# Linear attention followed by a gated MLP: state products paired with scores, normalisations on a second engine, and a new hand-written order

## The chip, the core and the metric

The kernel runs on one core of one Trainium2 chip. The metric is the device time of one execution in microseconds (us). The core's engines work side by side, each through its own list of instructions in order: TensorE (PE, matrix products and transposes into PSUM), VectorE (DVE), ScalarE (ACT), GpSimd (POOL, which has no way to PSUM) and SyncE (SP, which here only issues DMAs). Semaphores hold an instruction back until what it needs is done.

## What is computed

The reference takes q, k, v of 4 batches, 8 heads, 768 positions and 64 channels, and a decay per head, and computes linear attention in blocks of 64 positions; then, on the 512 channels of all heads, an MLP with a spatial gate:

```python
intra = ((qb @ kb.T) * Dmask) @ vb              # Dmask[i, j] = lam**(i-j) for i >= j, else 0
inter = (qb * lam_pow) @ kv_state
out[:, :, sl] = intra + inter
kv_state = lam_block * kv_state + (kb * rev_pow).T @ vb
...
h = np.maximum(x @ w_in, 0.0)                   # 512 -> 1024
u, v = h[..., :512], h[..., 512:]
v_n = (v - mean(v)) / np.sqrt(var(v) + 1e-06)   # per position, over the 512 channels
v_s = einsum('ts,bsd->btd', w_spatial, v_n) + b_spatial[None, :, None]
out = (u * v_s) @ w_out
```

## The kernel before

A batch of 768 positions is cut into three steps of 256; steps are numbered 0 to 11 over the four batches (n // 3 is the batch, n % 3 the step in it), and each step has two blocks of 128 (c = 0, 1). PSUM has eight banks; bank 7 holds the running state, the others are handed out by number.

**The order is written out by hand.** The string ORDER (lines 16 to 81) lists tokens such as `MK.3.1.3.4.D`: an operation, its indices, mostly its PSUM banks, and last the engine: T for TensorE, D for VectorE, A for ScalarE, P for GpSimd, S for SyncE's DMA queue. The loop at lines 526 to 528 issues them one after another, so a token's place in the string fixes its place in its engine's list; waits between engines follow from the data and the banks. Which engine makes a copy or an eviction is therefore a matter of the token's last letter.

The operations that this document speaks of, with the lines that the profile names:

- Loads by SP: LQ, LK, LV (line 190; three buffers each), BS the spatial bias, broadcast (258). Loads by GpSimd, cast to bf16 on the way: WI.0 and WI.1 the halves of w_in (246; WI.0 is the half for v, read by PV), WS.0 and WS.1 (251), WO (255). GT is a tiny copy on GpSimd that waits until a load has landed (242).
- Decay: KM, QM multiply k and q by their decay into bf16 (288); QC, VC only cast (177, 175 or 179, by engine); the last index of KM, QM, QC is the half, or 2 for the whole.
- Transposes: in steps 0 to 4 TK and TQ on PE (318), evicted by EK and EQ; from step 5 on by DMA, DK and DQ (301, 305).
- Scores SC (349): 16 products of 64x64 each for half of the channels, masked by MK on DVE (354). SC, KV and AV are the small products; all others on PE use the full array of 128x128.
- State products KV.n.c (366), 16 products into bank 7; SS copies the state out (177 or 175) before the next KV adds to it.
- Attention output AV.n.c (387 and 396): the part through the state copy, then scores times v. FN is a copy of one element that waits for the first half of AV. EX evicts the result (x) to SBUF.
- Projection: PV (421) gives the v half of a block of 128 positions, evicted with relu by EV; PU (459) gives the u half, evicted by EU.
- Normalisation: BN computes mean and variance on DVE (436, 437); RA takes the root on ACT (441), RD the reciprocal on DVE (446); VN subtracts the mean and scales, 128x512 bf16, on DVE (450).
- Spatial gate: WT transposes w_spatial on PE (471), EW evicts; GP writes the bias into a bank (481, shown at 175 or 177); PW (485) adds six products of 384 columns; GM multiplies by u on DVE (491).
- Output: PO (496), the last block in two halves PH (505), evicted by EO and EH, stored by ST and SH (519, 515).

The work of a batch overlaps the next: while the PW and PO of one batch run, the attention of the next batch is threaded between them.

Of the kernel before, what the change touches and what calls it, by code (L numbers as in the profile page):

```python
# [21 lines left out]
TK.2.0.6.T QC.2.0.A MK.1.1.0.1.D QC.2.1.D VC.1.A AV.0.0.2.3.T FN.0.2.3.A MK.1.0.4.5.D LV.2.S KV.1.0.T LK.3.S
KM.2.1.P TQ.2.0.0.T AV.1.0.1.4.T FN.1.1.4.A AV.0.1.2.3.T SS.1.0.D AV.1.1.1.4.T EX.1.1.4.A GT.1.2.P WS.1.P
TQ.2.1.5.T KV.1.1.T EX.1.0.1.D EX.0.1.3.D EX.0.0.2.D PV.1.1.4.T GT.2.1.P TK.2.1.1.T PV.0.0.3.T EV.1.1.4.A
EK.2.1.1.D PU.1.0.2.T PV.1.0.4.T LV.3.S BS.S EK.2.0.6.A SS.1.1.D EQ.2.0.0.D VC.2.D BN.1.1.D EQ.2.1.5.D KV.2.0.T
EV.0.0.3.A LQ.3.S BN.0.0.D EV.1.0.4.A SC.2.1.0.1.T EU.1.0.2.A BN.1.0.D RA.1.A SC.2.0.5.6.T MK.2.1.0.1.D KM.3.1.P
RD.1.D LK.4.S PU.0.1.3.T PV.0.1.4.T WT.0.0.2.T MK.2.0.5.6.D EV.0.1.4.A BN.0.1.D PU.1.1.0.T WT.2.0.1.T EU.0.1.3.A
SS.2.0.A AV.2.0.3.4.T RA.0.A EU.1.1.0.A WT.1.0.5.T FN.2.3.4.D AV.2.1.3.4.T LQ.4.S WT.0.1.6.T EW.2.0.1.D
EX.2.0.3.A WT.1.1.1.T EX.2.1.4.D EW.0.0.2.A EW.0.1.6.A PV.2.0.0.T PV.2.1.3.T VN.1.1.D EW.1.1.1.D RD.0.D LV.4.S
VN.0.1.D EW.1.0.5.A WO.P EV.2.0.0.D BN.2.0.D EV.2.1.3.A WT.2.1.4.T KM.3.0.P VC.3.A VN.1.0.D BN.2.1.D KM.4.0.P  # L30
PU.0.0.2.T RA.2.A TK.3.2.1.T GT.2.2.P PU.2.1.6.T VN.0.0.D RD.2.D EW.2.1.4.A KM.4.1.P GP.0.0.0.0.A GP.0.1.0.3.A
LQ.5.S KV.3.0.T VN.2.0.D LK.5.S PU.2.0.5.T VN.2.1.D PW.0.0.0.0.T EU.2.1.6.D GP.0.0.1.6.D EU.0.0.2.A GP.0.2.0.2.A
PW.0.1.0.3.T QC.4.2.P QC.3.2.D EU.2.0.5.D TQ.3.2.4.T PW.0.0.1.6.T EK.3.2.1.A GM.0.0.0.0.D QM.5.1.P PW.0.2.0.2.T
LQ.6.S GP.0.1.1.5.A GM.0.0.1.6.D LV.5.S EQ.3.2.4.D GP.0.3.1.0.A PW.0.3.1.0.T GM.0.1.0.3.D SS.3.0.D PW.0.1.1.5.T
GP.0.3.0.6.A GM.0.2.0.2.D SC.3.1.3.4.T KV.3.1.T GM.0.3.1.0.D MK.3.1.3.4.D SS.3.1.A GP.0.2.1.2.A SC.3.0.0.1.T
PW.0.3.0.6.T LK.6.S MK.3.0.0.1.D VC.4.P PW.0.2.1.2.T QM.5.0.P TQ.4.2.3.T GM.0.3.0.6.D QM.6.1.P TK.4.2.4.T
GM.0.2.1.2.D PO.0.2.0.T AV.3.0.1.6.T EQ.4.2.3.D KM.5.0.P GM.0.1.1.5.D KV.4.0.T EK.4.2.4.A EO.0.2.0.A FN.3.1.6.D
SC.4.0.2.3.T KM.5.1.P SS.4.0.A SC.4.1.4.5.T AV.3.1.1.6.T EX.3.0.1.D KV.4.1.T DQ.5.S MK.4.1.4.5.D EX.3.1.6.A
PO.0.4.0.T PV.3.1.6.T PV.3.0.1.T PO.0.3.4.T EV.3.1.6.A PU.3.0.5.T MK.4.0.2.3.D AV.4.0.2.6.T EV.3.0.1.A
EO.0.4.0.A VC.5.D BN.3.1.D KM.6.1.D FN.4.2.6.A DK.5.S BN.3.0.D SS.4.1.A EU.3.0.5.D LQ.7.S PO.0.5.3.T KM.6.0.P  # L40
LV.6.S EO.0.3.4.A AV.4.1.2.6.T KV.5.0.T EX.4.1.6.D EO.0.5.3.A LK.7.S QM.6.0.P SC.5.0.0.1.T SC.5.1.4.5.T
PO.0.1.3.T EX.4.0.2.A PV.4.1.2.T QM.7.1.P MK.5.0.0.1.D EO.0.1.3.A PV.4.0.6.T RA.3.A LV.7.S MK.5.1.4.5.D
AV.5.0.0.1.T GP.1.0.0.3.D EV.4.0.6.A VC.6.D FN.5.0.1.D SS.5.0.A PO.0.0.4.T KV.6.0.T EV.4.1.2.A AV.5.1.0.1.T
PU.4.1.5.T BN.4.0.D EX.5.1.1.A BN.4.1.D PU.4.0.6.T KM.7.1.D VC.7.D RD.3.D EX.5.0.0.A RA.4.A DQ.6.S DK.6.S
PV.5.1.2.T PV.5.0.1.T RD.4.D VN.4.1.D PU.3.1.0.T EU.4.0.6.A EV.5.1.2.A VN.3.0.D PU.5.1.6.T EU.4.1.5.D VN.4.0.D
QM.7.0.P EV.5.0.1.A BN.5.1.D EO.0.0.4.A BN.5.0.D SS.6.0.A EU.3.1.0.A DQ.7.S RA.5.A KM.7.0.P VN.3.1.D DK.7.S
SC.6.0.1.2.T KV.6.1.T RD.5.D SC.6.1.4.5.T LV.8.S VN.5.0.D VN.5.1.D PU.5.0.0.T LK.8.S EU.5.1.6.A MK.6.1.4.5.D
GP.1.2.1.6.A MK.6.0.1.2.D EU.5.0.0.A KM.8.1.P GP.1.1.1.0.A PW.1.2.1.6.T PW.1.0.0.3.T GP.1.3.1.4.A SS.6.1.D
PW.1.1.1.0.T LQ.8.S SC.7.0.1.2.T GM.1.2.1.6.D GM.1.0.0.3.D GM.1.1.1.0.D AV.6.0.5.6.T FN.6.5.6.D KV.7.0.T LQ.9.S
MK.7.0.1.2.D PW.1.3.1.4.T AV.6.1.5.6.T LK.9.S GP.1.0.1.3.D SS.7.0.A KV.7.1.T EX.6.0.5.A SC.7.1.0.1.T  # L50
PW.1.0.1.3.T QM.8.1.D MK.7.1.0.1.D GP.1.2.0.2.A GP.1.3.0.5.A KM.9.0.D PW.1.2.0.2.T PW.1.3.0.5.T GM.1.0.1.3.D
KM.8.0.P QM.8.0.P SS.7.1.A KM.9.1.P DK.8.S GM.1.2.0.2.D EX.6.1.6.A DQ.8.S GP.1.1.0.0.A GM.1.3.0.5.D LV.9.S
VC.8.A PW.1.1.0.0.T PV.6.0.1.T PV.6.1.6.T GM.1.3.1.4.D EV.6.0.1.A LK.10.S EV.6.1.6.A AV.7.0.2.3.T LK.11.S
SC.8.1.4.5.T GM.1.1.0.0.D SC.8.0.0.1.T FN.7.2.3.A MK.8.1.4.5.D KV.8.0.T AV.7.1.2.3.T EX.7.1.3.D MK.8.0.0.1.D
PO.1.5.6.T ST.0.0.S ST.0.3.S EX.7.0.2.A PU.6.1.4.T PO.1.4.5.T LQ.11.S BN.6.0.D AV.8.0.2.3.T VC.9.P PO.1.0.0.T
FN.8.2.3.D SS.8.0.D KV.9.0.T EO.1.4.5.D AV.8.1.2.3.T KM.10.1.P QM.9.1.D EU.6.1.4.A PV.7.1.1.T LQ.10.S EX.8.0.2.A
BN.6.1.D KM.10.0.P LV.10.S GP.2.3.1.4.D PU.7.1.5.T PV.7.0.2.T EV.7.1.1.D BN.7.1.D EX.8.1.3.A QM.9.0.P PV.8.0.3.T
RA.6.A RD.6.D DK.9.S EV.7.0.2.A EO.1.0.0.A PU.8.1.1.T SS.9.0.A PV.8.1.2.T EV.8.0.3.A VN.6.0.D BN.7.0.D
EV.8.1.2.A EO.1.5.6.A BN.8.0.D RA.7.A KV.9.1.T PU.6.0.0.T BN.8.1.D DQ.9.S VN.6.1.D GP.2.0.1.3.A QM.10.0.P
EU.6.0.0.A RD.7.D VN.7.1.D VN.7.0.D RA.8.A LV.11.S PO.1.1.2.T RD.8.D PO.1.2.6.T VC.10.P SS.9.1.D VN.8.0.D  # L60
VN.8.1.D QM.11.1.P PU.7.0.0.T QM.10.1.D EU.8.1.1.D EU.7.1.5.A PU.8.0.5.T EU.7.0.0.A EU.8.0.5.A GP.2.1.0.0.D
# [15 lines left out]
GP.3.3.1.4.A GM.3.2.1.0.D ST.2.4.S PW.3.3.1.4.T PW.3.1.1.2.T PW.3.2.0.3.T GP.3.0.0.6.D GM.3.3.1.4.D ST.2.2.S
GM.3.1.1.2.D PW.3.1.0.5.T PW.3.0.0.6.T PH.3.5.1.0.T GM.3.3.0.1.D GM.3.1.0.5.D one.D PO.3.4.4.T EO.3.4.4.A
PO.3.3.2.T GM.3.0.0.6.D GM.3.2.0.3.D ST.3.4.S EH.3.5.1.0.D PH.3.5.0.1.T EH.3.5.0.1.D EO.3.3.2.A PO.3.1.5.T
EO.3.1.5.D PO.3.0.6.T EO.3.0.6.D SH.3.5.1.S SH.3.5.0.S PO.3.2.3.T ST.3.3.S ST.3.1.S ST.3.0.S EO.3.2.3.A ST.3.2.S  # L80
# [478 lines left out]
```

## Time and profile before

| | |
|---|---|
| median of three runs | 148.28 us (147.71 to 148.53) |
| the profiled execution | 148.72 us, its span 147.0 us |
| mean granted TensorE clock | 0.971 |
| busy: PE, DVE, ACT, POOL | 130.0, 117.4, 75.7, 46.0 us |
| largest groups on PE | PW 33.0, PU 24.3, PV 23.9, PO 21.5 us |
| largest on DVE | MK 28.5, GM 16.4, BN 16.4, VN 10.9 us |
| HBM read, written | 24.77 MB, 6.29 MB |

The page gives one execution as the hardware profiler recorded it, times counted from its first instruction. A group line reads: source line, engine, operation, output<-inputs, shapes, count | busy time in us, mean ns of one | idle time of the engine just ahead of them and what ended it. The chain of waits goes back from the last instruction, at each step to what released it; a piece of it reads start, length, what. A line of waits reads: who waited, for whom, us in total, times, the longest. Helpers hide their callers: line 175 is every copy on ACT, 177 every copy on DVE, 426 and 428 every relu.

### The profile page before, as it was taken

The page shows a single profiled execution, that of the slowest core. Times are in us where ns is not written, and L with a number is a line of the kernel's source. Part 1 is how long each engine was busy: PE and PEld are TensorE (multiplying, and loading weights), DVE is VectorE, ACT ScalarE, POOL GpSimd, SP SyncE. Part 2 cuts the span into 40 slices and gives each one's busy share as a digit, 9 for nine tenths or more (in the row PEclk, how much of TensorE's full clock was granted, in tenths as well). Part 3 has the DMA queues.
Part 4 walks back from the last instruction along what each step waited for, and adds up shares of the span by engine and source line. Part 5 has one row for each costly group of instructions (what it writes and reads, how often), then busy time and mean ns, then how long its engine had stood idle before and what let it go on. Part 6 is the DMA issues. An engine that isn't in the chain of part 4 may idle for free.

```text
span 147.0 us, 4585 instructions
## 1 busy us (share of the span) xinstructions
PE 130.0 (88%) x1929; PEld 84.2 (57%) x1946; DVE 117.4 (80%) x229; ACT 75.7 (51%) x154; POOL 46.0 (31%) x57
## 2 busy tenths in 40 slices
PE   1077599999999999999999999996999899999990
PEld 1056364676766756477665656663664555865540
DVE  1289956799978789989997799899978779997640
ACT  3968323679862546468637414764506473580021
POOL 7669600240188670520048075373000000000000
PEclk9999955999999999999999999999999999999997
DMA  3999999999999677998995899992987386011065
GB/s 88 346 347 347 259 215 218 216 318 238 310 311 339 185 91 203 347 202 183 321 333 148 215 355 336 221 216 81 165 263 76 143 337 236 2 72 75 0 235 193
DMA packets 58374, 32.27 MB, mean 220 GB/s; under 512 B 15858, under 2 KB 55282, under 8 KB 58354
## 3 DMA queue, kind: packets, MB, share of 16 engines
q1 hardware_dynamic: 55968, 29.23, 73.0%
q0 software_dynamic: 2384, 2.75, 10.7%
q8 instruction: 15, 0.25, 0.7%
q14 instruction: 5, 0.04, 0.1%
q10 hardware_dynamic: 2, 0.00, 0.0%
HBM read 24.77 MB, written 6.29 MB: 211 GB/s over the span
## 4 chain that ended last, share of the span: by engine, by line
PE 80%; DMA 7%; SPq 5%; DVE 3%; issue 2%; ACT 1%; DVEq 0%
PE ps L485 22%; PE ps L459 15%; PE ps L421 14%; PE ps L496 12%; SPq L190 5%; DMA q_in<-in_q_dram 4%; PE ps L396 4%; PE ps L349 4%; PE ps L366 3%; PE ps L387 3%; DMA qT<-qc 3%; DVE a_sb L354 2%; PE ps L318 2%; PE ps L471 2%; PE ps L505 1%
## 5 line engine op out<-in xcount | busy, mean ns | idle before, releaser
L485 PE MATMUL ps<-wt_sb,vn 128*128 128x384 bf16 x192 | 33.0, 326 | 1.3 <-ACT ps L175 1.3
L354 DVE TENSOR_TENSOR a_sb<-ps,m 128x1024 bf16<-128x1024 f32 x24 | 28.5, 1214 | 2.8 <-PE ps L349 2.5
L288 POOL TENSOR_TENSOR kc<-k_in,lv 128x512 bf16<-128x512 f32 x17 | 19.0, 1131 | 35.2 <-DMA k_in<-in_k_dram 24.0
L485 PEld LDWEIGHTS <-vn 128*128 128x128 bf16 x192 | 18.3, 98 | 13.3 <-issue 1.5
L421 PE MATMUL ps<-win_sb,xT 128*128 128x512 bf16 x90 | 23.9, 399 | 0.7 <-issue 0.6
L459 PE MATMUL ps<-xT,win_sb 128*128 128x256 bf16 x192 | 24.3, 275 | 0.0
L496 PE MATMUL ps<-wout_sb,gT 128*128 128x512 bf16 x81 | 21.5, 380 | 0.8 <-issue 0.3
L459 PEld LDWEIGHTS <-win_sb 128*128 128x128 bf16 x192 | 18.5, 99 | 5.0 <-DMA win_sb<-in_moe_w_in_dram 0.6
L426 ACT ACTIVATE vh<-ps 128x512 bf16<-128x512 f32 x20 | 12.0, 599 | 14.6 <-PE ps L421 14.6
L491 DVE TENSOR_TENSOR gT<-ps,uT 128x384 bf16<-128x384 f32 x32 | 16.4, 547 | 3.1 <-PE ps L485 3.1
L175 ACT ACTIVATE o_sb<-ps 128x512 f32<-128x512 f32 x19 | 11.1, 593 | 14.4 <-PE ps L496 14.4
L436 DVE BATCH_NORM_STATS2 st<-vh 128x6 f32<-128x512 bf16 x24 | 16.4, 682 | 1.3 <-ACT vh L426 1.2
L288 POOL TENSOR_TENSOR qc<-q_in,lqn 128x512 bf16<-128x512 f32 x11 | 11.9, 1087 | 12.2 <-DMA q_in<-in_q_dram 5.1
L175 ACT ACTIVATE xT<-ps 128x512 bf16<-128x512 f32 x16 | 9.2, 596 | 11.6 <-PE ps L396 11.2
L421 PEld LDWEIGHTS <-xT 128*128 128x128 bf16 x96 | 9.4, 101 | 9.9 <-issue 0.8
L175 ACT ACTIVATE ps<-bsp 128x384 f32<-128x384 f32 x23 | 11.0, 491 | 5.3 <-DVE uT L428 2.7
L496 PEld LDWEIGHTS <-gT 128*128 128x128 bf16 x92 | 8.2, 98 | 8.2
L426 ACT ACTIVATE uT<-ps 128x512 bf16<-128x512 f32 x16 | 9.5, 593 | 4.2 <-PE ps L459 4.2
L450 DVE TENSOR_SCALAR vn<-vh,mv,rstd 128x512 bf16<-128x512 bf16 x24 | 10.9, 476 | 0.3
L396 PE MATMUL ps<-a_sb,vb 64*64 64x128 bf16 x384 | 10.2, 221 | 0.3 <-DVE a_sb L354 0.3
L349 PE MATMUL ps<-qT,kT 64*64 64x128 bf16 x384 | 9.2, 219 | 1.2 <-DVE a_sb L354 0.8
L366 PE MATMUL ps<-vb,kc 64*64 64x64 bf16 x320 | 8.7, 196 | 0.4 <-ACT seen L175 0.4
(70 smaller groups left out, 156.1 us busy)
## 6 DMA issues: line engine op xcount, KB each, us to landing
q_in<-in_q_dram SPq DMA_DIRECT2D x12, 512.0 KB, 6.6
k_in<-in_k_dram SPq DMA_DIRECT2D x12, 512.0 KB, 6.2
v_in<-in_v_dram SPq DMA_DIRECT2D x12, 512.0 KB, 6.0
out_dram<-o_sb SPq DMA_DIRECT2D x23, 256.0 KB, 2.8
wsp_raw<-in_moe_w_spatial_dram POOLq DMA_DIRECT2D x2, 576.0 KB, 15.9
win_sb<-in_moe_w_in_dram POOLq DMA_DIRECT2D x2, 512.0 KB, 11.4
wout_sb<-in_moe_w_out_dram POOLq DMA_DIRECT2D x1, 512.0 KB, 9.1
bsp<-in_moe_b_spatial_dram SPq DMA_DIRECT2D x1, 384.0 KB, 17.9
```

The source lines that it names most:

```text
L175: nc.scalar.activation(out=o, in_=i, func=AF.Copy)
L288: vec(e).tensor_tensor(out=dst[n % NCA][:, u].rearrange("p u m o d -> p o (u m) d"), in0=src[n % NIN].rearrange("p (o u) m d -> p o u m d" ...
L349: nc.tensor.matmul(out=pa[o][row(c), w, j], lhsT=kT[n % NTR][row(o), u, j, c * Q64:(c + 1) * Q64], rhs=qv(n, o, u, c), start=(w == 0 and j ...
L354: nc.vector.tensor_tensor(out=a_sb[n % NA][:, i].rearrange("p o w j x -> p o w (j x)"), in0=ps[:, b0:b1 + 1:b1 - b0].rearrange("p o (w y) ...
L396: nc.tensor.matmul(out=po[c ^ o][row(w), c, i], lhsT=vb[n % NCA][row(c), 4 * o + u, j, :], rhs=a[row(c), i, o, w, j, :], start=(r == 0 and ...
L421: nc.tensor.matmul(out=bank(b), lhsT=x[:, slot(c, g)], rhs=win_sb[:, g, DH:DFF], start=(g == 0), stop=(g == NCH - 1))
L426: nc.scalar.activation(out=o, in_=i, func=AF.Relu)
L436: nc.vector.bn_stats(out=st6[p2][:, t], in_=vh[p2][:, t])
L459: nc.tensor.matmul(out=pu[:, f2].rearrange("p (c x) -> p c x", c=2), lhsT=win_sb[:, g, f * P:(f + 1) * P], rhs=x[:, slot(0, g):slot(1, g) ...
L485: nc.tensor.matmul(out=bank(b)[:, 0:HW], lhsT=vn[bb % 2][:, s, f * P:(f + 1) * P], rhs=wt_sb[:, s, i * HW:(i + 1) * HW], start=False, stop ...
L491: nc.vector.tensor_tensor(out=gT[bb % 2][:, f, cols], in0=bank(b)[:, 0:HW], in1=uT[bb % 2][:, f, cols], op=ALU.mult)
L496: nc.tensor.matmul(out=bank(b), lhsT=gT[bb % 2][:, f, t * P:(t + 1) * P], rhs=wout_sb[:, f, :], start=(f == 0), stop=(f == NCH - 1))
```

## The change

Four things are edited.

1. A new operation KS takes the place of KV.n.0, KV.n.1 and one SC in steps 3, 4, 6, 7, 9 and 10. KS.n.c issues the 16 state products of block c and, between them, 8 of the 16 scores of channels half 0 (those that read the other half of the rows, o = 1 - c), so that two KS of a step replace two KV and SC.n.0.
2. VN gets a form for ACT: an activation with func Identity, scale rstd and bias shift, where shift = -mean * rstd comes from a new small operation NB on DVE (two values per partition and step). Eleven of the 24 VN go to ACT, 13 stay on DVE; eight NB are added.
3. f_l is rewritten: four products of the identity matrix with itself into a bank that is free. It was in the kernel before, but ORDER did not call it; now FL stands twice in the first steps. The memset of ones (token one, near the end) goes; its tile is renamed and no longer used.
4. ORDER is written anew throughout. Besides the places, engines change: five GP, three EV, two EO, two EK, two QC and one EW more on DVE; four VC, two EU, two EX, two SS, both EH and one QM fewer on it.

```diff
+    shift = many(2, [P, NT], FP32, "shift")
...
-    def f_l(e, k, w, b, new):
-        for i in range(k):
-            nc.tensor.matmul(out=bank(b)[:, 0:w], lhsT=ones[:, 0:P], rhs=ones[:, 0:w],
-                             start=(new == 1 and i == 0), stop=True, skip_group_check=True)
+    def f_l(e, n, b):
+        for i in range(4):
+            nc.tensor.matmul(out=bank(b)[:, 0:P], lhsT=ident, rhs=ident, start=True, stop=True)
...
+    def k_s(e, n, c, b0, b1):
+        pkv = bank(SB)[:, 0:4 * D].rearrange("p (u d) -> p u d", u=4)
+        new = n % NR == 0 and c == 0
+        o = 1 - c
+        ps_c = bank((b0, b1)[o]).rearrange("p (w j x) -> p w j x", w=2, j=2)
+
+        def state(u, m):
+            for h in range(2):
+                nc.tensor.matmul(out=pkv[row(h), u], lhsT=kc[n % NCA][row(c), u, m, h, :],
+                                 rhs=vb[n % NCA][row(c), 4 * h + u, m, :],
+                                 start=new and u == 0 and m == 0, stop=(u == 3 and m == 1),
+                                 skip_group_check=True)
+
+        for u in range(4):
+            w, j = divmod(u, 2)
+            for x in range(2):
+                nc.tensor.matmul(out=ps_c[row(x), w, j], lhsT=kT[n % NTR][row(o), w, j, x * Q64:(x + 1) * Q64],
+                                 rhs=qv(n, o, w, x), start=(u == 0), stop=(u == 3), skip_group_check=True)
+            state(u, 0)
+            state(u, 1)
...
+    def n_b(e, n):
+        r, p2 = n % NR, n // NR % 2
+        ts = slice(2 * r, 2 * r + 2)
+        nc.vector.scalar_tensor_tensor(out=shift[p2][:, ts], in0=mv[p2][:, ts, 0], scalar=-1.0,
+                                       in1=rstd[p2][:, ts], op0=ALU.mult, op1=ALU.mult)
+
     def v_n(e, n, c):
         t, p2 = 2 * (n % NR) + c, n // NR % 2
-        vec(e).tensor_scalar(out=vn[p2][:, t], in0=vh[p2][:, t], scalar1=mv[p2][:, t, 0:1],
-                             scalar2=rstd[p2][:, t:t + 1], op0=ALU.subtract, op1=ALU.mult)
+        if e == "A":
+            nc.scalar.activation(out=vn[p2][:, t], in_=vh[p2][:, t], func=AF.Identity,
+                                 bias=shift[p2][:, t:t + 1], scale=rstd[p2][:, t:t + 1])
+        else:
+            vec(e).tensor_scalar(out=vn[p2][:, t], in0=vh[p2][:, t], scalar1=mv[p2][:, t, 0:1],
+                                 scalar2=rstd[p2][:, t:t + 1], op0=ALU.subtract, op1=ALU.mult)
```

Of the order, the lists of some engines over the stretches that matter here, first before, then after (engine letters left out):

```text
SP   before  LQ.0 LQ.1 LK.0 LK.1 LV.0 LK.2 LQ.2 LV.1 LV.2 LK.3 LV.3 BS LQ.3 LK.4 LQ.4 LV.4 LQ.5 LK.5 ...
     after   LQ.0 LK.0 LQ.1 LK.1 LV.0 LV.1 LQ.2 LK.2 LV.2 LK.3 BS LK.5 LQ.3 LV.3 LK.4 LQ.4 LV.4 LQ.5 ...
POOL before  msk idn pos posk QC.0.1 QC.1.0 QC.1.1 QC.0.0 KM.1.1 GT.1.1 WI.0 WI.1 WS.0 KM.2.0 KM.2.1 GT.1.2 WS.1 ...
     after   msk idn posk pos QC.0.0 KM.1.0 WI.0 QC.1.1 WS.0 VC.1 GT.1.1 QC.2.1 WI.1 KM.2.0 WS.1 WO ...
PE   before  ... AV.1.1.1.4 TQ.2.1.5 KV.1.1 PV.1.1.4 TK.2.1.1 PV.0.0.3 PU.1.0.2 PV.1.0.4 KV.2.0 SC.2.1.0.1 ...
     after   ... AV.1.1.1.4 PV.0.1.5 FL.15.6 TK.2.1.3 PV.1.1.1 WT.0.0.0 SC.2.0.2.3 PV.1.0.4 PV.0.0.6 SC.2.1.0.1 PU.1.1.5 ...
PE   before  ... PU.2.0.5 PW.0.0.0.0 PW.0.1.0.3 TQ.3.2.4 PW.0.0.1.6 PW.0.2.0.2 PW.0.3.1.0 PW.0.1.1.5 SC.3.1.3.4 KV.3.1 SC.3.0.0.1 ...
     after   ... TK.3.2.6 PW.0.0.0.0 PW.0.2.1.5 TQ.3.2.3 PW.0.1.1.1 KS.3.0.5.6 SC.3.1.2.3 PW.0.3.1.4 PW.0.2.0.0 KS.3.1.5.6 TK.4.2.3 ...
ACT  after   ... RA.5 EU.5.1.3 VN.3.1 VN.5.1 VN.4.0 EU.3.1.3 EU.4.0.0 GP.1.0.0.3 ...
```

More of the change, by code (lines that the diff above doesn't have):

```diff
@@ L22 @@
[L22 to L61, printed above, removed]
@@ L77 @@
[L77 to L80, printed above, removed]
+LQ.0.S lam.A msk.P idn.P LK.0.S LQ.1.S mkc.D QC.0.1.D posk.P pos.P LB.0.T LN.0.A LL.D QC.0.0.P LK.1.S LX.A
@@ L147 @@
     bsp = sb([P, S], FP32, "bsp")
-    ones = sb([P, 512], BF16, "ones")
+    spare = sb([P, 512], BF16, "spare")
     q_in = many(NIN, [P, H, 2, D], FP32, "q_in")
@@ L519, in st_o @@
         eng.dma_start(out=out[bb, t * P:(t + 1) * P, :], in_=o_sb[(bb * NT + t) % NO])
-    ops = dict(GT=after, one=c_ones, FL=f_l, FN=f_n, lam=c_lam, posk=c_posk, pos=c_pos, LB=l_b, LN=l_n, LL=l_l, LX=l_x, LT=l_t, idn=c_ident, msk=c_mask, mkc=c_mask2, WI=w_in, WS=w_sp, WO=w_out, BS=b_sp,
+    ops = dict(GT=after, FL=f_l, FN=f_n, lam=c_lam, posk=c_posk, pos=c_pos, LB=l_b, LN=l_n, LL=l_l, LX=l_x, LT=l_t, idn=c_ident, msk=c_mask, mkc=c_mask2, WI=w_in, WS=w_sp, WO=w_out, BS=b_sp,
                LK=ld_k, LQ=ld_q, LV=ld_v, KM=k_m, QM=q_m, DK=d_k, DQ=d_q, QC=q_c, VC=v_c, TK=t_k, TQ=t_q, EK=e_k, EQ=e_q,
-               SC=s_c, MK=m_k, KV=k_v, SS=s_s, AV=a_v, EX=e_x, PV=p_v, EV=e_v, BN=b_n, RA=r_a, RD=r_d,
+               SC=s_c, MK=m_k, KV=k_v, KS=k_s, SS=s_s, AV=a_v, EX=e_x, PV=p_v, EV=e_v, BN=b_n, RA=r_a, RD=r_d, NB=n_b,
                VN=v_n, PU=p_u, EU=e_u, WT=w_t, EW=e_w, PW=p_w, GP=g_p, GM=g_m, PO=p_o, EO=e_o, ST=st_o, PH=p_h, EH=e_h, SH=s_h)
```

86 lines of the change are left out of this document (64 added, 22 removed).

## The prediction

> **What bounds the kernel now.** I read the page first, then the windows of ten microseconds, then the chain of waits.
>
> ```profile
> span 147.0 us, 4585 instructions
> PE 130.0 (88%) x1929; PEld 84.2 (57%) x1946; DVE 117.4 (80%) x229; ACT 75.7 (51%) x154; POOL 46.0 (31%) x57
> PE   1077599999999999999999999996999899999990
> ```
>
> The last line is the share of busy time in 40 slices of 3.7 us, in tenths: TensorE is idle or thin in the first five and nearly full afterwards. Two windows make that sharp:
>
> ```profile
> 20.00:30.00 10.00, 9.73 (x116) 5.76 (x111) 7.39 (x15) 4.86 (x8) 1.70 (x2) 0.71 1.17 217
> 40.00:140.00 100.00, 97.26 (x1419) 61.48 (x1432) 86.79 (x166) 49.39 (x103) 29.56 (x28) 1.00 0.77 202
> ```
>
> After the window's length stand the busy times of PE, weight loads, DVE, ACT and GpSimd, then PE's granted clock: 0.71 in the stretch from 20 to 30 us. From 40 to 140 us PE rests 2.7 us in 100, while DVE is 87% and ACT 49% busy. So PE is the bound there, and a new order can win at most those 2.7 us, unless PE's work itself becomes cheaper. The chain and the list of waits name where most of it lies:
>
> ```profile
> 98.84 2.07 PE ps L485 x12
> 100.91 0.68 DVE uT L428
> ...
> 101.61 0.50 ACT ps L175
> ...
> 110.33 4.00 DMA qT<-qc
> ```
> ```profile
> PE ps L485 <- ACT ps L175: 1.3, 1, 1.3
> PEld L459 <- DMA win_sb<-in_moe_w_in_dram: 0.6, 1, 0.6
> PE ps L349 <- DMA qT<-qc: 0.4, 1, 0.4
> ```
>
> PW.2.2.1 waits 1.3 us for a bias copy that ACT can make only after a late DVE eviction (EU.8.1), and the scores of step 11 wait 0.4 us for a transposing DMA. The other 1.0 us is scattered. Before 40 us the order of arrival of the inputs counts.
>
> **PE's own work (KS, and the regrouping).** These are the prices, from the chain of waits (start, length, what):
>
> ```profile
> 30.02 0.34 PE ps L471 x6
> ...
> 36.76 0.45 PE ps L318 x8
> 37.21 0.87 PE ps L459 x8
> 38.08 0.37 PE ps L366 x16
> 38.45 0.98 PE ps L459 x8
> ...
> 52.89 1.73 PE ps L421 x8
> ...
> 74.17 0.22 PE ps L396 x16
> 74.39 0.24 PE ps L366 x16
> ...
> 82.85 0.45 PE ps L349 x32
> ```
>
> A KV alone between full 128x128 products takes 0.37 us, inside a run of small 64x64 products 0.24; and the projection that follows takes 0.98 where its like takes 0.87. So each run of small products costs 0.13 + 0.11, about 0.22 us, for going in and out. 16 score products take 0.225 (0.45 for 32).
>
> From the first PW to the end, before has 14 KV, 18 SC and 17 runs of small products; after has 3 KV, 12 SC, 12 KS and 22 runs; the rest is the same piece for piece. A KS holds the 16 products of a KV and 8 scores. The trace has none. Bounds: if scores and states hide each other, the longer of the two, 0.24; if they simply add, 0.24 + 0.11 = 0.35; if every product starts at the pace of the lone KV, 24 x 0.37/16 = 0.56. Scores read one half of the rows and state products the other, as the two halves of an AV do, whose 16 products take 0.22, 14 ns each; that row is the nearest, so I take 0.25. Then: -11 x 0.24 - 6 x 0.225 + 12 x 0.25 = -1.0, and 5 more runs x 0.22 = +1.1. **Sum: +0.1 us**, with ends at -0.0 and +3.8. What the pairing saves, the splitting into more runs pays back.
>
> A KS adds a wait: the second of a step (KS.n.1) needs the state copy SS.n.0 of the first, and holds back half the scores, so MK.n.0 on DVE and whatever PE has queued behind. Between the two stand 0.6 (step 4) to 1.2 us of PE work, against one copy:
>
> ```profile
> L175 ACT ACTIVATE s_sb<-ps 128x256 bf16<-128x256 f32 x12 | 4.6, 379 | 5.2 <-PE ps L366 3.0 <-DVE seen L177 2.2
> L450 DVE TENSOR_SCALAR vn<-vh,mv,rstd 128x512 bf16<-128x512 bf16 x24 | 10.9, 476 | 0.3
> L222 ACT ACTIVATE lq<-posq,llrow 128x256 bf16<-128x256 f32 x12 | 5.0, 495 | 0.0
> L175 ACT ACTIVATE qc<-q_in 128x512 bf16<-128x512 f32 x1 | 0.6, 622 | 0.0
> L177 DVE COPY ps<-bsp 128x384 f32<-128x384 f32 x9 | 5.0, 551 | 0.1
> L177 DVE CAST vb<-v_in 128x1024 bf16<-128x1024 f32 x6 | 4.1, 686 | 1.0 <-DMA v_in<-in_v_dram 0.6 <-issue 0.5
> L428 DVE TENSOR_SCALAR vh<-ps 128x512 bf16<-128x512 f32 x4 | 2.7, 685 | 0.2 <-PE ps L421 0.2
> L436 DVE BATCH_NORM_STATS2 st<-vh 128x6 f32<-128x512 bf16 x24 | 16.4, 682 | 1.3 <-ACT vh L426 1.2
> L441 ACT ACTIVATE rstd<-mv,eps_t 128x2 f32<-128x2 f32 x12 | 3.5, 295 | 2.4 <-DVE mv L437 1.4 <-DVE seen L177 0.8
> ```
>
> 0.38 us and its hand-over fit, except in step 4, where perhaps 0.1 shows.
>
> **Eleven normalisations on ACT, and the other swaps.** A VN on DVE costs 0.476 on average, so DVE loses 5.2 us. On ACT it is a pass over 512 elements (0.62, the qc row) with two operands that differ per partition; one such operand costs about 0.495 - 0.379 = 0.12 (lq against s_sb, 256 elements each), so 0.62 + 0.23 = 0.85 is my estimate, 9.4 us for eleven; bounds 0.62 and 1.0.
>
> The Trainium skill ("ScalarE: Activation LUTs", Rules for kernel authors) says to put multiply and add on VectorE and not on ScalarE, against this edit; from the prices of its section What ACT_TABLE_LOAD costs, 186 ns, 93 for each such operand and 0.833 per element, an estimate is 799 ns, which makes the third rival below a little less likely than my 0.85 does. No row here shows the operation.
>
> Besides, DVE loses four VC (0.686 each, -2.7) and gains five GP (0.551, +2.8) and three EV (0.685, +2.1); the smaller swaps and eight NB (tiny: 0.3 at most, the RA row) come to about -1, so DVE ends some 4 us lighter and ACT about 7 heavier (9.4 less the five GP and three EV, plus small ones), 83 of 147 us. Neither is the bound on average, so I cost this at nothing by itself; what it buys is that DVE runs late less often. The cover is thin at the batch turn: in the second batch ACT must do VN.3.1, VN.5.1, VN.4.0, EU.3.1, EU.4.0 and GP.1.0.0 in a row before PW.1.0.0 can start (third rival).
>
> **The start.** Here GpSimd's queue sets when the weights are asked for:
>
> ```profile
> 9.48 1.04 POOL L288 TENSOR_TENSOR kc<-k_in,lv 128x512 bf16<-128x512 f32 x1 [1.43 <-DMA k_in<-in_k_dram]
> 10.46 0.64 POOL L242 COPY seen<-q_in 1x1 f32<-1x1 f32 x1
> 11.05 2.01 POOL L246 DMA_DIRECT2D win_sb<-in_moe_w_in_dram  x2
> 13.05 0.75 POOL L251 DMA_DIRECT2D wsp_raw<-in_moe_w_spatial_dram  x1
> ```
> ```profile
> DMA to landing us min/median/max: 10.2/11.4/12.6
> ```
> ```profile
> DMA to landing us min/median/max: 15.5/15.9/16.3
> ```
> ```profile
> 7.83 5.99 DMA q_in<-in_q_dram
> ```
> ```profile
> 16.97 1.22 DVE L354 TENSOR_TENSOR a_sb<-ps,m 128x1024 bf16<-128x1024 f32 x1
> ```
> ```profile
> 21.30 0.61 PE L421 MATMUL ps<-win_sb,xT 128*128 128x512 bf16 x1
> ```
>
> The two rows of landing are those of win_sb and wsp_raw; the last three are the third q load (from the chain), the last MK of steps 0 and 1, and the first projection. The weights arrive one after another: WI.0 at 11.05 + 10.2 = 21.3, WI.1 at 12.3 + 12.6 = 24.9 (where PU waited its 0.6), WS.0 at 13.05 + 15.5 = 28.6 or a little later, WS.1 near 32. Afterwards KM.1.0 still waits for the second k load (fourth in SP's queue in both), but the copy of 0.6 us is no longer ahead of WI.0, so the stream starts 0.6 us earlier, in the order WI.0, WS.0, WI.1, WS.1: 20.7, 24.7, 28.0, 31.5. The first projection, which began at 21.3, can begin near 20.9. LK.0, now second in SP's queue, brings the first scores forward, but on DVE QC.2.0 stands ahead of three of the four MK and waits for LQ.2, seventh load in both orders, landed at 7.83 + 5.99 = 13.8: two short copies (0.4 each) and three MK (1.2) end at 18.2, as before (16.97 + 1.22). WI.1 now comes third, and PU.1.1 needs it. PE arrives there after four PV (3.5), WT, TK, FL and two SC in two runs (1.7): 26.1 at full clock. The 0.71 row is 2.9 us lost, 0.65 of it ahead of 21.3; with the other 2.2 PE arrives at 28.3. So PU.1.1 starts at 28.0 to 28.5: the late weights hide behind the half clock, or take its place. From there to the first PW: 6 PU (5.2), 5 WT (1.7), 2 PV (1.7), KV and two AV (24 products at 14 ns) in two runs (1.4), TK (0.45): 10.5, hence 38.5 to 39.0, with the last weights at 31.5 just in time for WT.1.1. In before the first PW follows at 38.45 + 0.98 = 39.4. Two arrivals are only just in time, so I take the smaller end: **gain 0.4 us**, bounds +0.8 (a later stream) and -0.9 (nothing waits). The two FL cost 0.2 each and lie in this stretch.
>
> SP's queue also puts LK.5 ahead of LQ.3, LV.3 and LK.4, and LV.3 behind the bias load BS.
>
> ```profile
> 40.00 1.60 POOL L288 TENSOR_TENSOR kc<-k_in,lv 128x512 bf16<-128x512 f32 x1 [8.83 <-DMA k_in<-in_k_dram]
> ```
>
> KM.4.0 waited for LK.4 until 40.0. With one load more ahead, some 1.5 us (LK.1, fourth, was there at 9.48, LQ.2, seventh, at 13.8: 1.45 a load), it starts near 41.5 and KM.4.1 ends at 43.6; PE reaches TK.4 after five PW, TQ, SC and two KS, 6.4 us from 38.8, at 45.2. LV.3 lands one load sooner, its VC ends near 41.1, and KS.3.0 comes at 42.3. Both cost nothing while PE is not over 1.2 us early.
>
> **Waits that go.** EU.8.1 moves to ACT, and the third PW of that batch takes a bank that MK.9.0 frees with 3.7 us of PE work (PU, PO, two PW) left; DQ.11, which overwrites the qT that AV.9.1 reads, has 7.3 us of PE work between AV.9.1 and SC.11 where it had 3.5 (three PO and a PV), against the 4.0 that it took. So both named waits (1.7) should vanish; for what comes late instead I allow 0.6, SS in step 4 and a GM in front of SC.4.1 among it. **-1.1 us**, bounds -2.0 and +2.
>
> **Sum.** -0.4 + 0.1 - 1.1 = -1.4: a span of 145.6. The profiled execution took 148.72 for a span of 147.0, so 1.7 lies around it, and 147.3 would be the same execution; the median of the three runs, 148.28, lies 0.4 below it, so I forecast **146.9**. The end is untouched: the last product, its eviction on ACT and its store.
>
> **Rivals.**
> - Waits are traded one for one: DVE is 87% busy, and a new order has its own near misses; only the start's 0.4 less 0.1 is left: 148.0. For it: from the first PW on the new order has five places where less than 0.8 us of PE work lies between a product and the one that needs its eviction, the old one four. Against: DVE is 4 us lighter.
> - The pairing does nothing: scores and states add up, KS 0.35, 12 x 0.10 = 1.2 of the 1.4 is gone: 148.1.
> - Slower: ACT becomes the bound at the turn into PW. From the end of PV.5.1 to PW.1.0.0 PE has 6.9 us of work (four PU, a PO, a PW, SC, two KS and an AV in three runs); in that time stand EV 0.6, two BN 1.4 and their second halves 0.3, RA 0.3, and on ACT an EU 0.5, three VN at 0.77 (0.85 less overlap), two EU 1.0 and the GP 0.4: 6.8. From 0.8 per VN on PE waits, and where ACT and DVE come 1.2 us late at each of the three turns, 3.6 are lost: 150.5.
> - Slower by PE: products start singly. At 0.56 per KS, 12 x 0.31 = 3.7 are lost: 150.6. The Trainium skill ("TensorE: Matmul & The Clock Gate", Wait — 56ns, not 53.3ns?) puts a floor of about 25 ns under the distance of two matmuls; by it a KS takes 0.6. The 14 ns of the AV row speak against it.
>
> **Chances.** Forecast 0.50; traded waits 0.19; no pairing 0.09; ACT late 0.17; single starts 0.05. About 0.5%, 0.74 us, is what a measurement of this kernel can tell from no change, so between 147.5 and 149.0 it is the same: the second and third cases, less a little that falls below. Faster 0.51, same 0.26, slower 0.23. The forecast's own range is 146.2 to 147.5. The whole range leaves out most of the slow cases at the top and the case without any waits at the bottom: 145.2 to 149.6.
>
> **What would show it.** Right: a chain without a piece of DVE or ACT between two PW; the first PW at 38.4 to 39.1; KS steps of 0.24 to 0.28 between starts; VN on ACT at 0.8 to 0.9; DVE's busy time near 113, ACT's near 82. Wrong: PE waiting for ACT vn or for a GP behind it (third rival), for wsp_raw or win_sb between 22 and 32 us (the weights' new order), for SS inside a KS pair, or a half clock that lasts past 28 us.

## The result, and the profile after

| | before | after |
|---|---|---|
| median of 18 runs | 148.03 us (147.11 to 149.44) | 147.01 us (146.08 to 147.67) |
| ratio after / before | | 0.9935, 95% interval 0.9914 to 0.9956 |
| profiled execution, its span | 148.72, 147.0 us | 147.23, 145.5 us |
| first PW starts | 39.27 us | 37.70 us |
| from there to the last eviction | 104.0 us | 104.1 us |

The change makes the kernel faster by 1.0 us; 146.9 was forecast. A ratio leaves out the runs that lie over 1.5% above the same kernel's fastest; a median is of all runs.

The page of the changed kernel, first lines, then its share of busy PE time in 40 slices:

```profile
span 145.5 us, 4623 instructions
PE 130.7 (90%) x1938; PEld 84.2 (58%) x1954; DVE 113.3 (78%) x227; ACT 81.1 (56%) x161; POOL 46.8 (32%) x59
PE   1269999899999996999999999999999999999990
```

DVE and ACT stand where the forecast put them (113 and 82). PE is full from the fourth slice on, before from the sixth. The same two windows as before (length, PE, weight loads, DVE, ACT, GpSimd, granted clock, busy share of the DMA engines, GB/s):

```profile
20.00:30.00 10.00, 9.15 (x180) 5.85 (x172) 7.78 (x16) 6.36 (x11) 1.04 (x1) 1.00 1.17 216
40.00:140.00 100.00, 97.36 (x1432) 60.61 (x1444) 83.64 (x164) 53.35 (x107) 29.75 (x31) 1.00 0.85 206
```

From 20 to 30 us the clock is 1.00 instead of 0.71. From 40 to 140 us PE rests 2.64 us, against 2.74 before: there next to nothing was won. The list of waits and the chain say what rests instead:

```profile
PE ps L347 <- DMA qT<-qc: 1.1, 1, 1.1
PE ps L488 <- DMA win_sb<-in_moe_w_in_dram: 0.6, 1, 0.6
```
```profile
14.74 12.27 DMA win_sb<-in_moe_w_in_dram
27.06 1.05 PE ps L488 x8
...
48.05 0.07 DVE seen L179
48.11 0.41 PE ps L347 x16
...
50.13 6.12 DMA qT<-qc
56.25 0.04 issue
56.29 0.64 PE ps L347 x32
...
141.77 0.60 ACT o_sb L177
```

The wait for the bias copy (1.3) and that of step 11 (0.4) are gone. In their place the scores of step 5 (L347) wait 1.1 us for their own transposing DMA, which took 6.1 us from its issue to its landing. The last row is the last eviction, at 143.24 in before.

One execution of each kernel isn't enough to split 1 us, so both were profiled again (before_again, after_again, below). The first PW starts at 39.27 and 38.74 in before, at 37.70 and 38.27 after: 1.0 us earlier in the mean. From there to the last eviction it takes 104.0 and 103.0 before, 104.1 and 103.3 after: the same within 0.2 in the mean. **In these four profiles the whole gain lies ahead of the first PW.**

### The profile page after: what moved, and what is told of

Same layout as the page of the kernel before. It is cut to its first block, busy times and chain, and to the rows that moved or that the text cites. A ratio compares the mean times of both kernels' runs of the same rounds, so it can differ in the third digit from the quotient of the medians.

```text
span 145.5 us, 4623 instructions
## 1 busy us (share of the span) xinstructions
PE 130.7 (90%) x1938; PEld 84.2 (58%) x1954; DVE 113.3 (78%) x227; ACT 81.1 (56%) x161; POOL 46.8 (32%) x59
## 4 chain that ended last, share of the span: by engine, by line
PE 61%; DMA 22%; POOL 4%; DVE 4%; issue 2%; SPq 2%; ACT 2%; POOLq 0%
PE ps L514 17%; PE ps L525 13%; PE ps L488 11%; PE ps L440 10%; DMA k_in<-in_k_dram 9%; DMA win_sb<-in_moe_w_in_dram 8%; DMA qT<-qc 4%; PE ps L415 3%; PE ps L347 2%; SPq L192 2%; PE ps L406 2%; DVE a_sb L352 2%; POOL kc L286 2%; ACT vn L476 1%; POOL qc L181 1%
## 5 line engine op out<-in xcount | busy, mean ns | idle before, releaser
L514 PE MATMUL ps<-wt_sb,vn 128*128 128x384 bf16 x192 | 34.2, 326 | 0.0
L286 POOL TENSOR_TENSOR kc<-k_in,lv 128x512 bf16<-128x512 f32 x17 | 17.6, 1044 | 27.2 <-PE ps L377 11.7
L440 PE MATMUL ps<-win_sb,xT 128*128 128x512 bf16 x91 | 22.9, 379 | 0.5 <-issue 0.2
L520 DVE TENSOR_TENSOR gT<-ps,uT 128x384 bf16<-128x384 f32 x32 | 17.1, 549 | 4.3 <-PE ps L514 3.5
L177 ACT ACTIVATE o_sb<-ps 128x512 f32<-128x512 f32 (+1 forms) x19 | 10.7, 570 | 11.7 <-PE ps L525 11.2
L445 ACT ACTIVATE vh<-ps 128x512 bf16<-128x512 f32 x17 | 10.1, 592 | 10.4 <-PE ps L440 10.3
L181 POOL CAST vb<-v_in 128x1024 bf16<-128x1024 f32 x6 | 6.2, 1038 | 18.9 <-DMA v_in<-in_v_dram 13.7
L177 ACT ACTIVATE ps<-bsp 128x384 f32<-128x384 f32 x18 | 8.6, 494 | 2.9 <-DVE a_sb L352 1.9
L347 PE MATMUL ps<-qT,kT 64*64 64x128 bf16 x288 | 8.2, 240 | 2.0 <-DMA qT<-qc 1.1
L476 ACT ACTIVATE vn<-vh,shift,rstd 128x512 bf16<-128x512 bf16 x11 | 8.5, 807 | 1.7 <-DVE shift L470 1.7
```

Source lines behind the costliest of these rows:

```text
L177: nc.scalar.activation(out=o, in_=i, func=AF.Copy)
L286: vec(e).tensor_tensor(out=dst[n % NCA][:, u].rearrange("p u m o d -> p o (u m) d"), in0=src[n % NIN].rearrange("p (o u) m d -> p o u m d" ...
L347: nc.tensor.matmul(out=pa[o][row(c), w, j], lhsT=kT[n % NTR][row(o), u, j, c * Q64:(c + 1) * Q64], rhs=qv(n, o, u, c), start=(w == 0 and j ...
L440: nc.tensor.matmul(out=bank(b), lhsT=x[:, slot(c, g)], rhs=win_sb[:, g, DH:DFF], start=(g == 0), stop=(g == NCH - 1))
L445: nc.scalar.activation(out=o, in_=i, func=AF.Relu)
L514: nc.tensor.matmul(out=bank(b)[:, 0:HW], lhsT=vn[bb % 2][:, s, f * P:(f + 1) * P], rhs=wt_sb[:, s, i * HW:(i + 1) * HW], start=False, stop ...
```

## The experiments

Every ratio is to the kernel before, run beside it on the same chip.

### The kernels themselves, once more

> The kernel before, unchanged, for a second profile of its start. Theory (weights): whatever the clock does, the first PW comes within 0.2 us of 39.2, because TensorE waits for the last weights at WT.1.1 near 33.2. Rival (clock): the first PW moves by 0.5 us or more with the place of the half clock.

147.27 us, one run. The first PW came at 38.74, half a microsecond earlier than in the first profile, with the half clock there too, but from 17.2 to 24.0 us where the first profile had it from 19.0 to 25.8, so 1.8 us earlier. That speaks for the rival: the clock's place moves the start. The two waits that the change was to remove were smaller here, 0.4 us for the bias copy and 0.3 in step 11.

> The changed kernel, unchanged, as the measure for the three beside it and for a second profile. The first PW at 37.6 to 38.7 (five looks at this start lay there), a wait of SC.5 of 0.7 to 1.3 us; ratio to the kernel before 0.991 to 0.996.

147.27 us (147.04 to 147.55), ratio 0.9920 (0.9891 to 0.9949); as expected. The chain again holds the DMA of step 5; the list of waits gives PE 0.6 us for it here (0.77 from the end of one group to the start of the next, where the first profile has 1.25), since PE comes there later:

```profile
49.92 6.17 DMA qT<-qc
56.10 0.04 issue
56.14 0.64 PE ps L347 x32
```

The DMA lands at nearly the same time in both (56.25 and 56.10), though the first PW came 0.57 us apart. So in these two an earlier start is partly taken back at this place; in after_no_spare, below, it landed at 57.49.

### The start: clock, weights, or both

```
before_fill:  + FL.6.6 x3 ahead of SC.1.0.4.5, x1 ahead of TK.2.0.6; + FL.1.1 x3 ahead of AV.1.0.1.4
              (f_l taken from the changed kernel)
before_early: - GT.1.1.P WI.0.P WI.1.P     + WI.0.P WI.1.P GT.1.1.P
before_both:  both edits
```

> The kernel before, with seven groups of four spare 128-wide products (identity times identity, into a bank that holds nothing) put into TensorE's pauses between 13.7 and 18.2 us. Theory (clock): the kernel before lost its start to the half clock from 18.9 to 25.6 us, which follows a stretch in which TensorE was only about half busy; with the pauses filled the half clock goes or shrinks. The first projection stays at 21.3, then PU.1.0 waits for WI.1 until about 24.9, and the first PW comes some 0.5 us earlier than 39.27, at 38.7; time ratio 0.996 to 0.998. Rival (order): the half clock comes from elsewhere or is covered by the weights' arrival; the first PW stays within 0.2 us of 39.27, ratio 0.999 to 1.002.

148.41 us, ratio 1.0042 (1.0015 to 1.007). The half clock was gone, and yet the first PW came at 39.14. The rows of the timeline say why: four products of 512 columns now take 1.04 us (22.41) where before took 1.91 (23.41), and then PE waits for the weights.

```profile
22.41 1.04 PE L420 MATMUL ps<-win_sb,xT 128*128 128x512 bf16 x4
24.92 1.05 PE L458 MATMUL ps<-xT,win_sb 128*128 128x256 bf16 x8 [1.48 <-DMA win_sb<-in_moe_w_in_dram]
```

So in before the half clock was covered by the weights, as the rival had it; at 32.85 PE waits another 0.46 us for the last half of w_spatial. That the kernel became slower fits neither range of ratios, and why it did isn't shown.

> The kernel before with one edit on GpSimd: the small copy that waits for the second q load (GT.1.1, 0.64 us) goes behind the two weight loads WI.0 and WI.1 instead of ahead of them, so that the weights are asked for some 0.6 us earlier, in the old order. Theory (weights): the last of them lands near 31.3 instead of 31.9, and the first PW comes 0.3 to 0.6 us earlier than 39.2; ratio to the kernel before 0.996 to 0.998. Rival (clock or TensorE's work binds the start): first PW within 0.15 us of 39.2, ratio 0.999 to 1.001.

148.94 us, ratio 1.0073 (1.0035 to 1.0111). The last weights were asked for at 16.64 and landed 14.0 to 14.3 us later, before 31.0, where before had 32.2. The first PW came at 39.57: products ran at half pace until some 25.5 us, over the first projections (four of 512 columns still took 1.61 us at 24.30), and nothing waited for weights. The theory of the weights alone falls too. The first PW and the ratio lie outside what either expectation allowed, and what makes the whole 1.1 us slower isn't shown.

> The kernel before with both edits of its start: the spare products of before_fill and the earlier weights of before_early. Theory (two limits side by side): each alone left the other in place, both together move the first PW from about 39.1 to 37.7 to 38.3; ratio to the kernel before 0.992 to 0.996 if nothing later swallows it. Rival (something else binds the start, or the gain is lost behind it): first PW within 0.3 us of 39.1, or a ratio of 0.998 or more with waits after 40 us that before had not.

149.38 us, ratio 1.0055 (1.0018 to 1.0091), above the theory's range and on the rival's side. The profiled execution took 150.82 us, 1.4 above the median, and how much of its wait the other runs have isn't known. In it PE had done all its work ahead of the first PW by 38.66, 0.8 us earlier than before, and then the first PW waited for a third limit until 40.41:

```profile
40.41 0.81 PE L484 MATMUL ps<-wt_sb,vn 128*128 128x384 bf16 x4 [1.75 <-ACT ps L175]
```
```profile
36.89 1.24 DVE L449 TENSOR_SCALAR vn<-vh,mv,rstd 128x512 bf16<-128x512 bf16 x1
```

The bias copy on ACT stands behind the root of step 2, that behind the statistics on DVE, and those behind a normalisation that took 1.24 us instead of 0.41. GpSimd was at a product meanwhile (36.94 for 1.04 us). The clock and the weights are each a limit when the other is out of the way, but curing both in the old order doesn't bring the gain: a third stood right behind. In the changed order products run at full pace from 23.2 us at the latest, and there is 0.6 us at most of waiting for the weights and no wait of the first PW; how much of the 1.0 us each of the three brings isn't shown.

```
after_no_spare: - FL.4.6.T   - FL.15.6.T
```

> The changed kernel without its two groups of spare products. Theory (clock): the group at 15.4 us keeps TensorE busy through a pause; without it the full clock comes later than 20.1 us or is lost again, and the first PW comes 0.5 to 1.5 us later than 37.70; ratio to the kernel before 0.997 to 1.003. Rival (order): the denser order alone holds the clock and the spare products only fill a wait; the first PW stays within 0.2 us of 37.70, ratio 0.992 to 0.995.

146.2 us (145.8 to 150.1), ratio 0.9899 (0.9851 to 0.9947), faster than the rival's 0.992 to 0.995; first PW at 37.63. The spare products bring nothing that can be measured; the denser order alone holds the clock. The profiled execution is the longest, of 150.1 us: there the DMA of step 5 landed at 57.49, PE waited 2.1 us for it, and then the granted clock read 0.50 from 60 to 62 us, though PE was busy throughout. So the half clock came back behind that wait. Six more profiles of kernels whose order is the same up to there, but for the engine of the normalisations in one (after_again, after_split, after_norm_dve, after_dq5, its repetition and after_dq5_split), have the first PW at 37.85 to 38.65, by where the full clock sets in.

### The pairing

```
after_split:  - KS.n.0   + KV.n.0          (n = 3, 4, 6, 7, 9, 10)
              - KS.n.1   + SC.n.0 KV.n.1
```

> The changed kernel with each of the six pairs taken apart: KS.n.0 becomes the state products KV.n.0, and KS.n.1 becomes the scores SC.n.0 followed by KV.n.1, in the same places. Theory (pairing pays): a KS takes 0.25 us, so a step's three pieces 0.24 + 0.225 + 0.24 take 0.2 us more than two KS, six steps 1.2 us; ratio to the kernel before 0.999 to 1.003. Rival (nothing): TensorE waits at those places anyway and the split is absorbed; ratio 0.992 to 0.995.

147.52 us (147.15 to 148.25), ratio 0.9982 (0.9955 to 1.0008): between the two. Beside the changed kernel's ratios, 0.9935 and 0.9920, that is 0.7 to 0.9 us slower, with intervals of 0.3 to 0.4 us either way; by the medians (147.01 and 147.27, other chips) 0.25 to 0.5. PE's busy time says where the rest went:

```profile
40.00:140.00 100.00, 98.68 (x1438) 62.18 (x1451) 85.26 (x165) 54.24 (x110) 30.17 (x31) 1.00 0.84 205
```

PE is 1.3 us busier there than in the first profile of the changed kernel, and the wait of SC.5 is gone: with two steps' worth, some 0.4 us, more work ahead of it, and a first PW at 38.65, PE comes no earlier than the DMA. But a window that holds fewer waits is busier in any case, so the price of the pairs is read from the first PW to the last eviction: PE is busy there for 102.30 us, against 101.39 and 101.22 in the two profiles of the changed kernel and 101.03 and 101.10 in those of after_dq5. So the pairing saves PE some 0.9 to 1.3 us, near the 1.2 of theory; the changed kernel spends a part of them waiting.

### The wait of step 5

```
after_dq5:  - DK.5.S ... LQ.6.S ... DQ.5.S     + DK.5.S DQ.5.S ... LQ.6.S
```

> The changed kernel with one DMA moved: the transposing DMA of q in step 5 goes ahead of the load LQ.6, right behind that of k. Theory (a wait with one cause): it lands some 2 us earlier, before 55.2 us, the wait of SC.5 (1.25 us) goes, and nothing takes its place; ratio to the kernel before 0.985 to 0.987. Rival (waits are traded): LQ.6 and what hangs on it come later, and a wait of about the same size shows up by step 6 or 7; ratio 0.992 to 0.995.

146.51 us (145.67 to 148.83, and one run of 265.46, as one of 267.89 of the kernel before beside it), ratio 0.9894 (0.9852 to 0.9936), between the two ranges expected; a span of 144.5. The wait is gone; PE is busy 9.95 us from 50 to 60, where it had 8.87:

```profile
50.00:60.00 10.00, 9.95 (x162) 5.68 (x162) 9.11 (x15) 4.65 (x10) 5.19 (x5) 1.00 1.01 250
```

SP's queue was held 2.48 us by a transposing DMA there (at 53.16), and DVE had done its normalisations just before GpSimd came:

```profile
62.89 0.69 DVE L177 CAST vb<-v_in 128x1024 bf16<-128x1024 f32 x1 [0.81 <-DMA v_in<-in_v_dram]
...
67.01 0.15 DVE L468 SCALAR_TENSOR_TENSOR shift<-mv,rstd 128x2 f32<-128x2 f32 x1
```
```profile
67.43 2.04 POOL L284 TENSOR_TENSOR kc<-k_in,lv 128x512 bf16<-128x512 f32 x2 [5.29 <-PE ps L375]
```

The interval of the ratio overlaps that of the changed kernel, so it was run again.

> The kernel of after_dq5 again, since its first interval was wide. Theory (the wait has one cause and nothing takes its place): 0.5 to 1.2 us faster than the changed kernel beside it, ratio to the kernel before 0.985 to 0.990. Rival (traded): as the changed kernel, 0.991 to 0.995.

Its profiled execution took 146.19 us (span 144.5), but ten runs fall into two groups: four from 146.2 to 148.0, six from 151.0 to 152.4; the median of all is 151.0. The ratio, 0.9917 (0.9864 to 0.9971), is of the lower four. None of the 24 runs of the changed kernel lies above 147.7. The mean granted clock is 0.996 to 1.000 in the four and 0.983 to 0.989 in the six, as if these held a stretch of half clock of 3 to 5 us; no profile shows where.

> The kernel of after_dq5 with the six pairs taken apart as in after_split, so that the wait of SC.5 cannot hide what the pairing saves. Theory (a KS takes 0.25 us): 1.2 to 1.4 us slower than after_dq5 beside it, near 147.7 us. Rival (PE's work is not the bound there): less than 0.5 us slower.

150.24 us (146.9 to 151.7), in three groups: two runs at 146.9 and 147.7, four from 149.0 to 149.5, all with a mean granted clock of 1.000, and six from 151.0 to 151.7 with 0.983 to 0.989. The ratio, 1.0001 (0.9948 to 1.0054), takes two runs of the first group and two of the second, so that it can't be set beside after_dq5's: what the pairing saves isn't settled by this run. This time the profiled execution (151.34 us) was of the upper group. There PE waits 2.45 us from 69.59 for the mask product of step 6, and the timelines of DVE and of GpSimd show why:

```profile
67.65 1.23 DVE L477 TENSOR_SCALAR vn<-vh,mv,rstd 128x512 bf16<-128x512 bf16 x1
...
68.88 1.05 DVE L477 TENSOR_SCALAR vn<-vh,mv,rstd 128x512 bf16<-128x512 bf16 x1
69.86 0.99 DVE L468 SCALAR_TENSOR_TENSOR shift<-mv,rstd 128x2 f32<-128x2 f32 x1
70.77 1.21 DVE L350 TENSOR_TENSOR a_sb<-ps,m 128x1024 bf16<-128x1024 f32 x1
```
```profile
67.69 2.09 POOL L284 TENSOR_TENSOR kc<-k_in,lv 128x512 bf16<-128x512 f32 x2 [2.96 <-PE ps L362]
69.75 2.09 POOL L284 TENSOR_TENSOR qc<-q_in,lqn 128x512 bf16<-128x512 f32 x2
```

The same stretch of after_again:

```profile
66.81 0.41 DVE L479 TENSOR_SCALAR vn<-vh,mv,rstd 128x512 bf16<-128x512 bf16 x1
...
67.53 0.39 DVE L479 TENSOR_SCALAR vn<-vh,mv,rstd 128x512 bf16<-128x512 bf16 x1
67.84 0.15 DVE L470 SCALAR_TENSOR_TENSOR shift<-mv,rstd 128x2 f32<-128x2 f32 x1
68.09 1.23 DVE L352 TENSOR_TENSOR a_sb<-ps,m 128x1024 bf16<-128x1024 f32 x1
```
```profile
68.25 2.04 POOL L286 TENSOR_TENSOR kc<-k_in,lv 128x512 bf16<-128x512 f32 x2 [5.65 <-PE ps L377]
```

In after_dq5_split each of the three DVE instructions that meet GpSimd ends just after one of GpSimd's ends (its rows hold two each, so 1.045 us apiece): 68.88 behind 68.73, 69.93 behind 69.78, 70.85 behind 70.80. A shift over two elements takes 0.99 us instead of 0.15. In the changed kernel GpSimd is released (by the last state product of step 6 on PE) 0.26 us after the last of them is done. The mask product, which reads PSUM, takes 1.2 us in both. How DVE came so late stands further up in SP's queue:

```profile
53.00 4.21 SPq L297
57.21 0.05 issue
57.27 0.57 SPq L190
57.84 0.04 issue
57.88 6.07 DMA v_in<-in_v_dram
```
```profile
63.69 1.04 POOL L284 TENSOR_TENSOR qc<-q_in,lqn 128x512 bf16<-128x512 f32 x1
```

Here a transposing DMA held SP's queue 4.2 us, and the v load behind it landed at 63.95. The cast of v, which takes 0.69 us in after_again, then took 1.30 beside this other GpSimd product, and the first normalisation began at 67.65 instead of 66.81. In after_better the picture is the same (the queue held 3.74 us, v at 63.5, the cast 1.30). In the two profiles of after_dq5 the wait of SC.5 is gone as well, yet there is no such meeting: the queue was held 2.48 and 2.62 us, v was there by 62.9, and DVE was done 0.25 to 0.27 us before GpSimd came, about as in the changed kernel. So taking the wait of SC.5 away isn't enough to bring the two together. In these profiles it took a late v load besides; the changed kernel, whose PE and so GpSimd come later, had v only at 63.7 in its first profile and escaped. Why the same DMA holds the queue 2.5 us in one execution and 4.2 in another stays open.

The wait is not all that the profiled execution of after_dq5_split pays. From about 72.9 to 76.4 products ran at half pace again, as after the wait in after_no_spare: six PW products took 1.92 us, where after_better, with a wait of 2.4 us and no half clock behind it, took 0.97. That is some 1.7 us on top of the wait:

```profile
73.08 1.92 PE ps L512 x6
```
```profile
72.55 0.97 PE ps L512 x6
```

The first row is after_dq5_split, the second after_better. With the granted clocks of the groups this makes three kinds of runs likely: without the pause, with it, and with it and the half clock. That the upper runs of after_dq5_again are the third kind is only argued.

### The normalisations

```
after_norm_dve:  VN.n.c.A -> VN.n.c.D (eleven);   - NB.n.D (eight)
```

> The changed kernel with all 24 normalisations on VectorE and without the eight small shift instructions; the order is otherwise the same. Theory (ACT buys DVE time): DVE gets some 4 us more (117 instead of 113), ACT 9 less (72), and DVE is late at one or two of the batch turns: 0.5 to 2 us slower than the changed kernel, ratio to the kernel before 0.997 to 1.007. Rival (no use): TensorE does not wait for either engine at those places, ratio 0.992 to 0.995.

149.66 us (149.31 to 150.95), ratio 1.012 (1.0075 to 1.0164): 2.4 to 2.7 us slower than the changed kernel by the medians, 2.7 to 3.0 by the ratios, more than theory asked for. PE waits 0.3 and 0.4 us at the turn into the second batch and 1.6 at that into the third, where the chain holds DVE pieces in a row:

```profile
PE ps L511 <- DVE vn L476: 1.6, 1, 1.6
```
```profile
100.47 1.12 DVE a_sb L349
101.59 0.32 DVE vn L476
101.91 0.60 DVE uT L444
102.51 0.33 DVE vn L476
102.84 0.05 issue
```

So the largest effect that was measured on a single part of the change is that the normalisations before a PW leave DVE. The order around them is made for that; what the move is worth in the old order wasn't run.

### The three moves together

```
after_better:  after_dq5;   AV.3.1 ahead of SC.4.1;   WT.2.0 and KV.2.0 ahead of PU.1.1
```

> The changed kernel with three moves: the transposing DMA of q in step 5 ahead of the load LQ.6 (as in after_dq5); AV.3.1 ahead of SC.4.1, which waited 0.22 us for a VectorE product; the transposition WT.2.0 and KV.2.0 ahead of PU.1.1, which waited 0.65 us for WI.1. Theory: the waits of 1.25, 0.22 and up to 0.65 us go; in an execution whose clock comes late the third was not there; 145.2 to 146.2 us, ratio to the kernel before 0.982 to 0.988. Rival (traded): the gain of after_dq5 alone, ratio 0.989 to 0.991.

151.23 us (148.9 to 154.0), ratio 1.0132 (1.0071 to 1.0194) of the three lower runs of six: both expectations miss. The profiled execution is the lowest, 148.91 us. In it the three waits did go (first PW 37.92, none at SC.5), and then PE waited 2.4 us at 69.2 with the same collision as in after_dq5_split: a normalisation of 1.15 us from 67.22, beside GpSimd from 67.18. No version that beats the changed kernel reliably was found.

## Why the prediction came out, step by step

The time was right to 0.1 us, but that close only by luck. The forecast was 1.4 us off a median of three runs, 148.28; measured were 1.0 off 148.03. The start gained 0.6 us more than its term, the waits about 1.1 less than theirs, and the base lay 0.25 lower: two terms were wrong in opposite directions. What was right is the sign, the price of PE's work and that of the normalisations.

- **PE's own work, +0.1: right.** From the first PW to the last eviction PE is busy 101.19 and 101.22 us in the two profiles of before, 101.39 and 101.22 in those of the changed kernel: 0.1 more in the mean. Its working has a slip: 0.13 + 0.11 is 0.24 and not 0.22, five runs then cost 1.2 and the sum is +0.2. Where scores or state products follow a KS, the steps are 0.25, 0.25, 0.25 (and 0.47 with a wait); where a full-width product follows, 0.35, so 0.10 for going out; a PW ahead of small products takes 1.07 instead of 0.98. Neither KS rival holds. The chain shows the halves interleaved:

```profile
67.87 0.15 PE ps L385
68.02 0.04 PE ps L377 x3
68.05 0.03 PE ps L385
```

- **The start, 0.4: the mechanism partly right, the size wrong; it is 1.0.** The step charged the new order with 2.2 us of before's half clock, so that PE would reach PU.1.1 at 28.3 instead of 26.1. That half clock wasn't there: the full clock set in at 20.1 to 23.2 and held through the start, and PE reached PU.1.1 at 26.41 in the profiled execution. And the weights came sooner than the working had them: WI.1 at 27.0 instead of 28.0, the last at 16.55 + 14.1 = 30.65 instead of 31.5. PU.1.1 waited 0.65 us for WI.1, which the prediction named as a sign against it. What the step had wrong is the clock and the times of arrival; the gain lies just beyond its bound of 0.9 for "nothing waits".
- **Waits that go, -1.1: failed.** The two waits named did go. Their 1.7 us was that of one execution, though: in before_again the same two are 0.7 in all. The step allowed 0.6 for what would come late instead, and it was as much as what went: PE's idle time from the first PW to the last eviction is 2.78 and 1.81 us in before, 2.68 and 2.12 in the changed kernel. In it stand 0.6 to 1.1 at SC.5, 0.22 at SC.4.1 (the GM that the prediction named), 0.26 at PU.7.1, and 0.24 at TK.4 in one execution. For this part the rival "waits are traded" was the right one. The prediction followed SP's queue for the loads, but not for DQ.5, which the new order puts behind LQ.6.
- **SP's queue at TK.4, nothing: nearly right.** KM.4.0 started at 42.56 instead of 41.5, and TK.4, reached at 44.20, waited 0.24.
- **Normalisations on ACT: right in price and in place.** 0.807 us each, below the 0.85 taken (the prices of the Trainium skill, "ScalarE: Activation LUTs", What ACT_TABLE_LOAD costs, gave 799 ns, which the trace bears out within 1%); no PW waited for one. Rival three did not come. That the step was costed "at nothing by itself" hid what it is worth: after_norm_dve shows 2.4 us or more.

```profile
L476 ACT ACTIVATE vn<-vh,shift,rstd 128x512 bf16<-128x512 bf16 x11 | 8.5, 807 | 1.7 <-DVE shift L470 1.7
L479 DVE TENSOR_SCALAR vn<-vh,mv,rstd 128x512 bf16<-128x512 bf16 x13 | 5.2, 430 | 0.0
```

## What to carry to other kernels

When PE is 97% busy, count which waits the new order makes, by the same care as those it removes: follow every DMA that PE will need through its queue. An earlier start is worth only as much as the next arrival lets through, here that of the DMA of step 5. A wait may add to the slack that keeps two other engines apart, so look at what is released sooner before you take one away. And profile a kernel twice before you split a difference of 1 us: the two waits that this forecast counted on were 1.7 us in one execution and 0.7 in the next.
